# Attention with a long convolution beside it on one core: bounds in pairs, transform results copied whole, a fourth vector exponential, another order at the end

## The chip, the cores and the metric

The kernel runs on one core of one Trainium2 chip. The metric is the time on the device of one execution, in microseconds; the time of a kernel is the median of its runs. Engines: TensorE (PE for its matmuls, PEld for its weight loads), VectorE (DVE), ScalarE (ACT), GpSimd (POOL) and SyncE (SP); the last two mostly issue DMAs here.

## The reference

Two independent parts, each 2048 rows by 512 columns, side by side in the output:

```python
# A: attention, 32 heads of 16, one K and V for all heads
q = (x @ wq).reshape(B, S, H, Dh).transpose(0, 2, 1, 3)
k = x @ wk
v = x @ wv
scores = jnp.einsum("bhqd,bkd->bhqk", q, k) * (Dh ** -0.5)
o = jnp.einsum("bhqk,bkd->bhqd", softmax(scores), v)
a = o.transpose(0, 2, 1, 3).reshape(B, S, H * Dh) @ wo
# B: a causal convolution of 4 taps, a product, a causal convolution over
# the whole sequence (by transforms of length 4096), a gate
kv = shift(k, shift_k) * v
y = irfft(rfft(pad(kv)) * rfft(pad(ssm_k)))[:S] + kv * ssm_D
b = q * y
out = concatenate([a, b], axis=-1)
```

## The kernel before

**Attention.** The 32 heads times 2048 queries are cut into 32 stacks (`NQ`), numbered n: four heads and a chunk of 512 queries each. For a stack the kernel goes over 16 tiles of 128 keys (`NKT`), two heads of the stack at a time, so there are 32 turns to a stack. A turn emits the scores of one pair (`keys`, L934, eight matmuls in float16), the exponential of the pair on ScalarE (`exp`, L946, 128 partitions by 1024) and, later, the products with the values (`pv`, L970), which add up in PSUM over the stack. A turn of `attend` works two pairs ahead with scores and exponentials. The last stack goes through half its queries first, then the other half. At the end of a stack VectorE copies the two accumulators out (L979, L980), and the rows are stored; `heads` loads them back with the row sums (`rl`), takes reciprocals, spreads them through a DMA (`r`) and divides (L1076 to L1088); `wo_part` multiplies by `wo`. For stacks 30 and 31 the division is done in place by `over` (L1190 to L1201, six VectorE operations), and `last` writes the last rows of the output.

**The vector exponential.** For the stacks in `OWN_IN` the last key tile isn't given to ScalarE. Its scores go to PSUM, and VectorE makes the exponential by a polynomial (`own`): two reads of the scores for each of two head pairs (L1022, L1023), then for each pair one conversion (L1030) and five steps (L1033). TensorE then takes the values' products from there (L970, `f<-own`). Each such stack saves ScalarE two exponentials.

**The rest as fillers.** All other work (the projections of the queries, their bounds, the convolutions, the output projection) is cut into pieces by eight generator threads. Between the scores of two turns `_Fill.turn` puts in pieces as a small table of prices lets it: a turn has a budget of TensorE time (`SLOT` 916, `SCORES` 220, `PV` 430, `UNIT` 216 ns per unit of filler) and of VectorE time (each turn adds `RATE` 850 to a credit, and every piece takes its stated price off it). Groups of filler matmuls are two turns apart (`GAP`). A thread that comes earlier in the list is served first; `own` is the first. So the program is written in one order, and each engine works down its own list: a matmul that waits holds back all matmuls behind it. A piece that asks a different price, or is cut differently, moves every piece behind it.

**PSUM.** The scores use two pairs of banks, and another two pairs (`f`) hold one stack's accumulators and one filler group. A filler group can begin when VectorE has read the group before it.

**Transforms of the convolution.** `forward` (L284 to L289) and `backward` (L440 to L469) multiply by tables (`ft`: `ff` forward, `fi` backward) that GpSimd loads from memory a little ahead (`in_ff`, `in_fi`). Each group fills two banks, and VectorE copies or multiplies them out, one bank at a time.

**Bounds.** The exponentials are shifted by a bound made from the queries' size: for each of four groups of heads and each of four query chunks one matmul (L707) into 32 rows of a bank, a scaling (`gn`, L709), a maximum (`gm`, L729), and a DMA to the queries' rows in memory.

## Time and profile before

| | |
|---|---|
| median of 3 runs | 1016.74 us (1013.69 to 1018.21) |
| the profiled execution | 1014.1 us |
| its span | 1012.3 us |
| mean granted TensorE clock | 0.989 |
| TensorE matmuls, busy | 947.4 us, 94% |
| ScalarE, busy | 953.3 us, 94% |
| VectorE, busy | 738.7 us, 73% |
| GpSimd, busy | 172.0 us, 17% |

The profile is one execution. A group of instructions is told as line, engine, operation, output tile<-input tiles, count, then busy time and mean length of one, then the engine's idle time just before them with what ended it. In a row of a wait the numbers are the total, the times and the longest. In a row of a stretch they are its length, then the busy time (and count) of PE, PEld, DVE, ACT and POOL, the granted TensorE clock (1 is full speed), the share of the DMA engines and GB/s. In a row of the timeline they are start, length, engine and line; "[3.42 <-DMA ff<-in_ff]" says that the engine was idle for 3.42 us and that this load ended it.

### The profile page before, as it was taken

The page shows a single profiled execution, that of the slowest core. Times are in us where ns is not written, and L with a number is a line of the kernel's source. Part 1 is how long each engine was busy: PE and PEld are TensorE (multiplying, and loading weights), DVE is VectorE, ACT ScalarE, POOL GpSimd, SP SyncE. Part 2 cuts the span into 40 slices and gives each one's busy share as a digit, 9 for nine tenths or more (in the row PEclk, how much of TensorE's full clock was granted, in tenths as well). Part 3 has the DMA queues.
Part 4 walks back from the last instruction along what each step waited for, and adds up shares of the span by engine and source line. Part 5 has one row for each costly group of instructions (what it writes and reads, how often), then busy time and mean ns, then how long its engine had stood idle before and what let it go on. Part 6 is the DMA issues. An engine that isn't in the chain of part 4 may idle for free.

```text
span 1012.3 us, 51279 instructions
## 1 busy us (share of the span) xinstructions
PE 947.4 (94%) x23439; PEld 463.1 (46%) x23439; DVE 738.7 (73%) x1009; ACT 953.3 (94%) x1034; POOL 172.0 (17%) x305
## 2 busy tenths in 40 slices
PE   8999999999999999999999989999889989998985
PEld 4344455444454444445554545544334445443452
DVE  4647866998538888989988858598999942866633
ACT  4699999999999999999999989999999999999982
POOL 2443111411003000101233434000000023200000
PEclk9899999999999999999999999999999999999998
DMA  7262333432123211122154424101211143310101
GB/s 231 92 190 75 119 103 102 107 99 84 46 75 78 70 53 54 53 90 75 55 152 123 126 86 124 54 22 47 70 37 43 42 126 115 92 56 25 42 4 46
DMA packets 69317, 83.12 MB, mean 82 GB/s; under 512 B 20800, under 2 KB 58278, under 8 KB 69094
## 3 DMA queue, kind: packets, MB, share of 16 engines
q1 hardware_dynamic: 47142, 43.51, 13.6%
q0 software_dynamic: 20320, 35.46, 11.8%
q8 instruction: 185, 3.03, 1.3%
q10 hardware_dynamic: 1632, 0.81, 0.3%
q14 instruction: 38, 0.31, 0.1%
HBM read 54.66 MB, written 25.03 MB: 79 GB/s over the span
## 4 chain that ended last, share of the span: by engine, by line
PE 56%; ACT 27%; DVE 9%; issue 7%; DMA 2%; POOL 0%; SPq 0%; ACTq 0%; DVEq 0%; POOLq 0%
ACT p L946 26%; PE f L970 26%; PE s L934 16%; PE f L249 12%; DVE own L1033 2%; DVE sp L169 1%; DMA xb<-in_A_x 1%; DVE ao L979 1%; PE x L231 0%; PE f L617 0%; DVE u L218 0%; DVE sp L289 0%; DVE sp L219 0%; DVE sp L220 0%; DVE ao L980 0%
## 5 line engine op out<-in xcount | busy, mean ns | idle before, releaser
L946 ACT ACTIVATE p<-s 128x1024 f32<-128x1024 f32 x1018 | 940.8, 1068 | 22.2 <-PE s L934 19.3
L970 PE MATMUL f<-p,vx 64*32 64x512 f32 (+1 forms) x8896 | 554.0, 556 | 1.7 <-DVE cut L683 1.1
L934 PE MATMUL s<-st,kst 49*32 49x512 f16 x8144 | 431.0, 382 | 31.2 <-ACT p L946 27.6
L934 PEld LDWEIGHTS <-kst 49*32 49x32 f16 x8192 | 199.0, 89 | 396.5 <-issue 355.4
L970 PEld LDWEIGHTS f<-p,vx 64*32 64x32 f32 x8896 | 178.3, 106 | 30.0 <-issue 4.3
L169 DVE TENSOR_TENSOR sp<-sp 128x1024 f32<-128x1024 f32 x96 | 111.3, 1214 | 0.0
L289 DVE COPY sp<-f 128x512 f32<-128x512 f32 x64 | 41.2, 685 | 63.8 <-PE f L249 63.8
L294 POOL DMA_DIRECT2D ff<-in_ff x64 | 34.5, 544 | 284.4 <-ACT p L946 282.1
L249 PE MATMUL f<-wo,o 64*32 64x512 f16 x1440 | 57.4, 375 | 3.8 <-DVE r L467 1.6
L979 DVE COPY ao<-f 128x512 f32<-128x512 f32 (+1 forms) x33 | 22.2, 673 | 50.3 <-PE f L970 50.3
L169 DVE TENSOR_TENSOR sp<-sp,sp 128x1024 f32<-128x1024 f32 x48 | 55.9, 1213 | 0.2
L249 PE MATMUL f<-xT,wq 64*32 64x512 f16 x1344 | 51.8, 375 | 1.6 <-DVE gm L729 1.3
L294 POOL DMA_DIRECT2D fi<-in_fi x32 | 17.6, 555 | 187.1 <-ACT p L946 187.1
L249 PE MATMUL f<-a,ff 64*32 64x256 f32 x1024 | 43.4, 382 | 4.6 <-DMA ff<-in_ff 3.4
L467 DVE TENSOR_TENSOR r<-f,q 128x256 f32<-128x256 f32 x32 | 12.1, 419 | 45.2 <-PE f L249 45.2
L249 PE MATMUL f<-hT,ff 64*32 64x256 f32 x1024 | 41.5, 377 | 1.2 <-PE s L934 0.3
L249 PE MATMUL f<-sp,fi 64*32 64x256 f32 x1024 | 40.4, 376 | 0.4 <-PE s L934 0.4
L469 POOL DMA_DIRECT2D out<-r x32 | 17.5, 552 | 106.2 <-DVE r L467 105.9
L404 DVE TENSOR_TENSOR a<-a,t 128x512 f32<-128x512 f32 x48 | 33.2, 691 | 1.6
L395 DVE TENSOR_TENSOR t<-kk,tpb 128x512 f32<-128x512 f32 (+1 forms) x50 | 32.9, 662 | 0.7 <-DMA qd<-qp 0.7
L249 PEld LDWEIGHTS <-o 64*32 64x32 f16 x1440 | 22.5, 93 | 19.0 <-DVE r L467 2.1
L322 POOL DMA_DIRECT2D hin<-in_B_ssm_k x32 | 21.1, 665 | 58.8 <-ACT p L946 57.4
(165 smaller groups left out, 726.5 us busy)
## 6 DMA issues: line engine op xcount, KB each, us to landing
ff<-in_ff POOLq DMA_DIRECT2D x64, 128.0 KB, 2.7
od<-ao SPq DMA_DIRECT2D x60, 128.0 KB
qd<-qp SPq DMA_DIRECT2D x48, 128.0 KB
st<-qd SPq DMA_DIRECT2D x62, 98.0 KB
kk<-in_B_k POOLq DMA_DIRECT2D x32, 128.0 KB, 3.0
v<-in_B_v POOLq DMA_DIRECT2D x32, 128.0 KB, 3.2
hin<-in_B_ssm_k POOLq DMA_DIRECT2D x32, 128.0 KB, 5.5
fi<-in_fi POOLq DMA_DIRECT2D x32, 128.0 KB, 3.4
```

Of the source, the lines that this page charges most:

```text
L169: v.tensor_tensor(part(out), part(a), part(b), op)
L249: y = self.nc.tensor.matmul(out[j : j + 32, cols], w[r, j : j + 32], x[r], start=half == m == 0, stop=half == 1 and m == k - 1,)
L289: self.nc.vector.tensor_copy(c[:, :, m + i, :], b[i].rearrange("p (q n) -> p q n", q=2))
L294: self.paced(self.nc.gpsimd.dma_start(t[:, i], self.I[n][:, 2 * m2 + i]))
L322: self.paced(nc.gpsimd.dma_start(dst, src))
L395: nc.vector.tensor_tensor(out[:, n], kk[:, x], tap(i, n.stop - n.start), ALU.mult)
L404: nc.vector.tensor_tensor(a, a, t, ALU.add)
L934: self.nc.tensor.matmul(s[j : j + 32, e, :], self.kst[rows, k * P + j : k * P + j + 32], self.st[n][rows, a, cols], start=True, stop=True,)
L946: self.exps[u % 4] = self.nc.scalar.activation(self.pt[u], s, AF.Exp, scale=LN2 * DH**-0.5 / SC / SC)
L970: nc.tensor.matmul(self.acc[e][32 * j : 32 * j + 32, m], vx[rows, :], y, start=k == 0, stop=stop)
L979: nc.vector.tensor_copy(a, self.acc[0][:, m])
L1033: v.scalar_tensor_tensor(g, g if i < 4 else y, c[i], y if i else x.bitcast(BF16), ALU.add, ALU.mult)
```

## The change

Four edits.

- `OWN_IN` has 27 as well, so four stacks have a vector exponential.
- `halves` keeps its pair of banks as `self.both`; `forward` copies both banks in one instruction (128x1024 in place of two of 128x512) and `backward` multiplies both in one (128x512 in place of two of 128x256).
- `bounds` takes a tuple of one or two head groups: two matmuls go to rows 0 to 31 and 32 to 63 of one bank, and one `gn` and one `gm` read both. There are nine calls instead of sixteen; the DMAs stay one for each group.
- The end: the divisions of stack 30 (`lt`, two halves) and of the first half of stack 31 (`lr`) move from `wo_part` to the end of the thread `own`, which is served first, with a smaller step between looks (`WAIT, 0.5`). `last` puts the first matmul of the last output rows ahead of the final two value products, adds row block 0 on TensorE by an identity matmul, copies blocks 0 and 2 by ScalarE, adds block 1 on VectorE, and makes and stores block 3 in two halves.

Since the prices of the pieces are met earlier or later, the fillers from turn 83 on stand at other turns than before. The names of lines shift by three or more in the new program (L1033 is L1036, L294 is L295, L1088 is L1104).

GpSimd's queue where the second short convolution begins (stack 18): `out<-r` stores of the backward transform, loads `kk` and `v`, first forward tables `ff`. Before, then now:

```order
L469 DMA out<-r_13277 128x256 x2
L373 DMA kk_11516<-in_B_k 128x256 x2
L386 DMA v_13407<-in_B_v 128x256 x2
L373 DMA kk_11516<-in_B_k 128x256 x2
L386 DMA v_13621<-in_B_v 128x256 x2
L469 DMA out<-r_13393 128x256 x2
L294 DMA ff_13671<-in_ff 128x256 x2
L294 DMA ff_13674<-in_ff 128x256 x2
```

```order
L469 DMA out<-r_13125 128x256 x2
L374 DMA kk_11675<-in_B_k 128x256 x2
L387 DMA v_13286<-in_B_v 128x256 x2
L469 DMA out<-r_13283 128x256 x2
L295 DMA ff_13403<-in_ff 128x256 x2
L295 DMA ff_13406<-in_ff 128x256 x2
```

The first `ff` load stands after one `kk` and `v` pair where there were two. In turns: its issue was at 593 and its first matmul at 594; now they are at 581 and 586.

VectorE in stack 28, from the end of the second read of the scores (`own` from `f`) to the last step; `ao` is the accumulator's read, `r` the gate of the backward transform. Before, then now:

```order
L1023 SCALAR_TENSOR_TENSOR own_16575<-own_16574,f_19925 128x1024
L1030 TENSOR_SCALAR x_19936<-own_16574 128x1024
L1033 SCALAR_TENSOR_TENSOR own_16574<-own_16575 128x1024
L1033 SCALAR_TENSOR_TENSOR own_16574<-own_16574,own_16575 128x1024 x3
L1033 SCALAR_TENSOR_TENSOR own_16574<-own_16574,x_19936 128x1024
L1030 TENSOR_SCALAR x_20081<-own_16574 128x1024
L467 TENSOR_TENSOR r_19823<-f_20000,q_19443 128x256 x2
L979 COPY ao_20159<-f_19590 128x512
L980 TENSOR_TENSOR ao_20159<-ao_20159,f_19590 128x512
L1033 SCALAR_TENSOR_TENSOR own_16574<-own_16575 128x1024
L1033 SCALAR_TENSOR_TENSOR own_16574<-own_16574,own_16575 128x1024 x3
L1033 SCALAR_TENSOR_TENSOR own_16574<-own_16574,x_20081 128x1024
```

```order
L1033 TENSOR_SCALAR x_19946<-own_10601 128x1024
L1036 SCALAR_TENSOR_TENSOR own_10601<-own_10602 128x1024
L1036 SCALAR_TENSOR_TENSOR own_10601<-own_10601,own_10602 128x1024 x2
L982 COPY ao_20078<-f_19559 128x512
L983 TENSOR_TENSOR ao_20078<-ao_20078,f_19559 128x512
L1036 SCALAR_TENSOR_TENSOR own_10601<-own_10601,own_10602 128x1024
L1036 SCALAR_TENSOR_TENSOR own_10601<-own_10601,x_19946 128x1024
L467 TENSOR_TENSOR r_19833<-f_20010,q_19190 128x512
L1033 TENSOR_SCALAR x_20096<-own_10601 128x1024
L1036 SCALAR_TENSOR_TENSOR own_10601<-own_10602 128x1024
L1036 SCALAR_TENSOR_TENSOR own_10601<-own_10601,own_10602 128x1024 x3
L1036 SCALAR_TENSOR_TENSOR own_10601<-own_10601,x_20096 128x1024
```

The accumulator's read stands earlier in the chain, and `r` is one instruction. The second read is written at turn 889 and the products with the chain's end at 906; before, at 887 and 906. In the other stacks: 29 had 925 and 944, now 921 and 940; 30 had 959 and 976, now 951 and 968; 27 now has 857 and 876.

VectorE in stack 31, where `ao` is the accumulator's read, `wp` the rows of the last output block (from the group that TensorE makes with `wo`), and `lr` the six operations of `over`. Before, then now:

```order
L1171 SCALAR_TENSOR_TENSOR wp_20716<-f_22217,wp_20716 128x512
L1171 SCALAR_TENSOR_TENSOR wp_20717<-f_22217,wp_20717 128x512
L1195 STREAM_TRANSPOSE lr<-ao_22064 128x256
L1197 TENSOR_SCALAR lr<-lr 128x8
L1198 RECIPROCAL lr<-lr 128x8
L1199 COPY lr<-lr 128x256
L1200 STREAM_TRANSPOSE lr<-lr 128x256
L1201 TENSOR_TENSOR lr<-ao_22064,lr 128x256
L1195 STREAM_TRANSPOSE lr<-ao_22064 128x256
```

```order
L982 COPY ao_22011<-f_21400 128x512
L983 TENSOR_TENSOR ao_22011<-ao_22011,f_21400 128x512
L1201 STREAM_TRANSPOSE lr<-ao_22011 128x256
L1203 TENSOR_SCALAR lr<-lr 128x8
L1204 RECIPROCAL lr<-lr 128x8
L1205 COPY lr<-lr 128x256
L1206 STREAM_TRANSPOSE lr<-lr 128x256
L1207 TENSOR_TENSOR lr<-ao_22011,lr 128x256
L1187 SCALAR_TENSOR_TENSOR wp_20593<-f_21975,wp_20593 128x512
L1187 SCALAR_TENSOR_TENSOR wp_20594<-f_21975,wp_20594 128x512
L1201 STREAM_TRANSPOSE lr<-ao_22011 128x256
```

Before, both halves of `over` stood behind the last `wp` read of the `wo` groups; now the first half stands ahead of the first of those reads and the second half behind it. In turns: 998 to 1000 before, with the reader on TensorE at 999; now 987 to 989, with the reader at 997. The division of the first half of stack 31 stood behind all four `wp` adds after that (L1184), and now stands ahead of them (turn 1002).

The diff:

```diff
--- before.py
+++ after.py
@@ -68,7 +68,7 @@
 
 DOWN = 80
 OWN = NKT - 1
-OWN_IN = (28, 29, 30)
+OWN_IN = (27, 28, 29, 30)
 OWN_AT, OWN_PV = 14, 8
 
 
@@ -240,6 +240,7 @@
                 start = not banks
                 if start:
                     f = self.pair()
+                    self.both = f
                     banks += [f[:, 0, :], f[:, 1, :]]
                 for m in range(n, n + g // grain):
                     for e in range(2):
@@ -285,8 +286,8 @@
 
         work = [[(slice(CB * q, CB * q + CB), ft[:, i, q, :], src[:, i, :]) for q in range(2)] for i in range(2)]
         b = yield from self.halves(*work, 2, 1400)
-        for i in range(2):
-            self.nc.vector.tensor_copy(c[:, :, m + i, :], b[i].rearrange("p (q n) -> p q n", q=2))
+        out = c[:, :, m : m + 2, :].rearrange("p q i n -> p i q n")
+        self.nc.vector.tensor_copy(out, self.both.rearrange("p i (q n) -> p i q n", q=2))
 
     def table(self, n, m2):
         t = self.w.tile([P, 2, 2, P], F32, tag="ft", bufs=FT, name=self.nm(n))
@@ -463,8 +464,7 @@
                     x = cx[:, cc, 4 * g2[m // 4] + g1[m % 4], :]
                     work[i].append((cols, ft[m2][:, i, cc, :], x))
             b = yield from self.halves(*work, 2, 850)
-            for i in range(2):
-                nc.vector.tensor_tensor(r[:, i, :], b[i][:, cols], q[m2][:, i, :], ALU.mult)
+            nc.vector.tensor_tensor(r, self.both[:, :, cols], q[m2], ALU.mult)
             for i in range(2):
                 nc.gpsimd.dma_start(self.orr[:, 2 * m2 + i, D + blk * CB : D + (blk + 1) * CB], r[:, i])
 
@@ -700,14 +700,17 @@
         for r, part in ((0, 0), (DH, 1), (BR + 1, 0)):
             self.nc.sync.dma_start(self.qd[8 * g : 8 * g + 8, r : r + DH, c * 512 : (c + 1) * 512], qp[:, part, :])
 
-    def bound(self, g, c, b):
+    def bound(self, gs, c, b):
 
 
         nc, w = self.nc, self.w
-        nc.tensor.matmul(b[0:32, :], self.wb, self.qa[g, c], start=True, stop=True)
-        gn = w.tile([8, 512], F16, tag="gn", bufs=3, name=self.nm("gn"))
-        nc.vector.tensor_scalar(gn, b[0:8, :], -1.02 * SC * SC / ONE, -60000.0, ALU.mult, ALU.max)
-        nc.sync.dma_start(self.qd[8 * g : 8 * g + 8, BR, c * 512 : (c + 1) * 512], gn)
+        n = 32 * len(gs)
+        for i, g in enumerate(gs):
+            nc.tensor.matmul(b[32 * i : 32 * i + 32, :], self.wb, self.qa[g, c], start=True, stop=True)
+        gn = w.tile([n - 24, 512], F16, tag="gn", bufs=3, name=self.nm("gn"))
+        nc.vector.tensor_scalar(gn, b[0 : n - 24, :], -1.02 * SC * SC / ONE, -60000.0, ALU.mult, ALU.max)
+        for i, g in enumerate(gs):
+            nc.sync.dma_start(self.qd[8 * g : 8 * g + 8, BR, c * 512 : (c + 1) * 512], gn[32 * i : 32 * i + 8])
 
     def first_bound(self, b, a):
 
@@ -725,8 +728,9 @@
             r = slice(BR + 64 * e, BR + 64 * e + 1)
             self.nc.vector.tensor_scalar(st[r, a, :], b[r, e, :], f, -60000.0, ALU.mult, ALU.max)
 
-    def bound_max(self, g, c, b):
-        self.nc.vector.tensor_reduce(self.gm[0:16, 4 * c + g : 4 * c + g + 1], b[0:16, :], AX.X, ALU.max)
+    def bound_max(self, gs, c, b):
+        n = 32 * len(gs) - 16
+        self.nc.vector.tensor_reduce(self.gm[0:n, 4 * c + gs[0] : 4 * c + gs[0] + 1], b[0:n, :], AX.X, ALU.max)
 
     def prologue(self):
         nc = self.nc
@@ -824,12 +828,12 @@
             return 4
         return 5 if any(self.step >= x and ("wo", 4 * c) not in self.seen for c, x in enumerate(WO_AT)) else None
 
-    def bounds(self, g, c):
+    def bounds(self, gs, c):
         yield 2, 1400, NEW, 2
         b = self.bank()
-        self.bound(g, c, b)
-        self.bound_max(g, c, b)
-        self.qs.add((g, c))
+        self.bound(gs, c, b)
+        self.bound_max(gs, c, b)
+        self.qs.update((g, c) for g in gs)
 
     def rest_of_q(self):
         for c in range(2, 4):
@@ -837,7 +841,7 @@
             b = self.bank()
             self.kv_rows(self.kvt, c, b)
             self.k_chunk(c, b)
-        yield from self.bounds(0, 0)
+        yield from self.bounds((0,), 0)
         work = [y for dk in range(4) for y in self.three(self.wq[1][:, :, dk, :], self.xT[0][:, :, dk, :])]
         n = 0
         while n < 12:
@@ -862,9 +866,8 @@
                     cut = [self.q_cut(x) for x in b]
                     for i in range(2):
                         yield from self.q_parts(g + i, c, cut[i])
-                for h in range(g + (c == g == 0), g + 2):
-                    yield WAIT, 2
-                    yield from self.bounds(h, c)
+                yield WAIT, 2
+                yield from self.bounds((1,) if c == g == 0 else (g, g + 1), c)
             if c == 0:
                 for g in range(4):
                     yield 0, 700
@@ -1033,6 +1036,19 @@
                     v.scalar_tensor_tensor(g, g if i < 4 else y, c[i], y if i else x.bitcast(BF16), ALU.add, ALU.mult)
             self.owed = [(-1 - n, part) for part in range(2)]
         self.seen.add("own")
+        yield from self.after(("cx", 1))
+        both = self.w.tile([P, 2, 4, 512], F32, tag="in", bufs=1, name="lr")
+        self.lt, self.lr = both[:, 0], both[:, 1]
+        while self.slot < 2 * NKT * (NQ - 1) + 1:
+            yield WAIT, 0.5
+        for h in range(2):
+            yield 0, 1800
+            self.over(self.ao2[:, 256 * h : 256 * h + 256], self.lt, h)
+        self.seen.add("lt")
+        while self.slot < 2 * NKT * (NQ - 1) + NKT:
+            yield WAIT, 0.5
+        yield 0, 1800
+        self.over(self.ao[:, 0:256], self.lr, 0)
 
     def attend(self, fill):
         self.od = self.dr.tile([NQ, P, 512], F32, name="od")
@@ -1169,23 +1185,13 @@
             b = yield from self.wo_rows(i, [14], 1400)
             for r in range(2):
                 nc.vector.scalar_tensor_tensor(self.wp[i + r], b[r], 1 / (OS * WS), self.wp[i + r], ALU.mult, ALU.add)
-        both = w.tile([P, 2, 4, 512], F32, tag="in", bufs=1, name="lr")
-        t, self.lr = both[:, 0], both[:, 1]
-        for h in range(2):
-            while self.slot < 2 * NKT * (NQ - 1) + 1:
-                yield WAIT, 1
-            yield 0, 1800
-            self.over(self.ao2[:, 256 * h : 256 * h + 256], t, h)
+        yield from self.after("lt")
         halves = [slice(256 * h, 256 * h + 256) for h in range(2)]
         for i in (0, 2):
-            work = [[(h, t[:, 2, r * P : (r + 1) * P], self.wl[0][:, h]) for h in halves] for r in (i, i + 1)]
+            work = [[(h, self.lt[:, 2, r * P : (r + 1) * P], self.wl[0][:, h]) for h in halves] for r in (i, i + 1)]
             b = yield from self.halves(*work, 2, 1400)
             for r in range(2):
                 nc.vector.tensor_tensor(self.wp[i + r], self.wp[i + r], b[r], ALU.add)
-        while self.slot < 2 * NKT * (NQ - 1) + NKT:
-            yield WAIT, 1
-        yield 0, 1800
-        self.over(self.ao[:, 0:256], self.lr, 0)
 
     def over(self, a, t, h):
 
@@ -1206,24 +1212,29 @@
         xr = self.out.rearrange("b (c p i) d -> (b c) p i d", c=4, p=P, i=4)
         fill.finish()
         t = self.w.tile([P, 2, 4, 512], F32, tag="big", bufs=2, name="lb")[:, 0]
-        self.pv(len(self.at) - 2, None)
-        s = [self.wide()[:, 0, :]]
         y = [self.s2("y", (512,)) for _ in range(4)]
         rows = lambda x, i: x[:, 2, i % 2 * P : (i % 2 + 1) * P]
-        self.mm(s[0], rows(self.lr, 0), self.wl[1])
+        b = self.pair()
+        s = [b[:, 0, :], b[:, 1, :]]
+        self.mm(s[0], rows(self.lr, 0), self.wl[1], stop=False)
+        self.pv(len(self.at) - 2, None)
         self.pv(len(self.at) - 1, None, True)
         self.over(self.ao[:, 256:512], t, 0)
-        s += [self.wide()[:, 0, :], self.wide()[:, 0, :], self.bank()]
+        self.mm(s[0], self.ident, self.wp[0], start=False)
         self.mm(s[1], rows(self.lr, 1), self.wl[1])
+        s += [self.wide()[:, 0, :], self.wide()]
         self.mm(s[2], self.ident, self.wp[2], stop=False)
-        for i in range(2, 4):
-            self.mm(s[i], rows(t, i), self.wl[1], start=i > 2)
-        for i in range(2):
-            nc.vector.tensor_tensor(y[i], self.wp[i], s[i], ALU.add)
+        self.mm(s[2], rows(t, 2), self.wl[1], start=False)
+        nc.scalar.copy(y[0], s[0])
+        nc.sync.dma_start(xr[3][:, 0, 0:D], y[0])
+        nc.vector.tensor_tensor(y[1], self.wp[1], s[1], ALU.add)
+        nc.sync.dma_start(xr[3][:, 1, 0:D], y[1])
         nc.scalar.copy(y[2], s[2])
-        nc.vector.tensor_tensor(y[3], self.wp[3], s[3], ALU.add)
-        for i in range(4):
-            (nc.sync, nc.scalar)[i // 2 % 2].dma_start(xr[3][:, i, 0:D], y[i])
+        nc.scalar.dma_start(xr[3][:, 2, 0:D], y[2])
+        for i, h in enumerate((slice(0, CB), slice(CB, D))):
+            self.mm(s[3][:, i, 0:CB], rows(t, 3), self.wl[1][:, h])
+            nc.vector.tensor_tensor(y[3][:, h], self.wp[3][:, h], s[3][:, i, 0:CB], ALU.add)
+            nc.sync.dma_start(xr[3][:, 3, h], y[3][:, h])
 
 
 class _Fill:
```

## The prediction

> **What bounds the kernel now.** I read the page first (busy shares, the chain of work that ended last, the costliest groups), then the waits of TensorE, then busy time by stretches, one stretch per stack, and last the timeline of the two places where the pace broke most.
>
> ```profile
> PE 947.4 (94%) x23439; PEld 463.1 (46%) x23439; DVE 738.7 (73%) x1009; ACT 953.3 (94%) x1034; POOL 172.0 (17%) x305
> PE 56%; ACT 27%; DVE 9%; issue 7%; DMA 2%; POOL 0%; SPq 0%; ACTq 0%; DVEq 0%; POOLq 0%
> L946 ACT ACTIVATE p<-s 128x1024 f32<-128x1024 f32 x1018 | 940.8, 1068 | 22.2 <-PE s L934 19.3
> ```
>
> ScalarE's 1018 exponentials set the pace: 940.8 us of busy time are 0.924 us each, 1068 ns long and overlapping their neighbours. Outside the start and the end ScalarE stood idle only 22.2 us, nearly all of it waiting for scores. TensorE is as busy (94%), but its matmuls are written in order and one that must wait blocks the scores behind it. So the body can lose time only by fewer exponentials or fewer waits of TensorE. These are the waits that matter, us in total, times, longest:
>
> ```profile
> PE f L249 <- DMA ff<-in_ff: 3.4, 1, 3.4
> PE x L231 <- issue: 2.5, 1, 2.5
> PE f L249 <- DVE gm L729: 2.3, 4, 1.0
> PE f L249 <- issue: 2.2, 1, 2.2
> PE f L249 <- DVE r L467: 1.6, 1, 1.6
> PE f L970 <- DVE cut L683: 1.1, 1, 1.1
> PE f L249 <- DVE wp L1140: 1.0, 1, 1.0
> PE f L970 <- DVE own L1033: 0.6, 1, 0.6
> ```
>
> By stretch (length, then busy PE, PEld, DVE, ACT, POOL, granted clock), the three stacks with a vector exponential (28, 29, 30), stack 31, and the stretch of stack 18 that holds the DMA wait:
>
> ```profile
> 872.20:901.80 29.60, 28.84 (x736) 14.58 (x721) 18.05 (x24) 29.55 (x33) 5.37 (x10) 1.00 0.27 82
> 901.80:932.80 31.00, 28.72 (x736) 13.46 (x736) 20.92 (x23) 29.56 (x34) 2.08 (x4) 1.00 0.08 26
> 932.80:963.50 30.70, 28.02 (x720) 13.17 (x719) 22.77 (x27) 29.77 (x33) 0.00 (x0) 1.00 0.17 46
> 963.50:993.30 29.80, 26.88 (x880) 16.84 (x864) 9.12 (x23) 26.20 (x29) 0.00 (x0) 0.94 0.02 4
> 575.00:600.00 25.00, 21.34 (x521) 11.88 (x512) 12.34 (x24) 20.15 (x22) 9.68 (x19) 0.93 0.34 106
> ```
>
> ScalarE idled 0.05, 1.44 and 0.93 us in the three stacks (2.4 together), 3.60 us in stack 31 and 4.85 us around 590.
>
> **One exponential fewer per round of keys.** Adding stack 27 to the list takes two exponentials off ScalarE, 2 x 0.92 = -1.8 us. TensorE's score and value matmuls of that tile stay; its 94% could cover the gain, but the row of stack 28, which already has the list's treatment, shows ScalarE 29.55 of 29.60, so ScalarE sets the pace there. Bounds -1.8 and 0.
>
> **What the added chain costs.** VectorE reads the two key groups and then runs twelve dependent operations, in stack 30:
>
> ```profile
> 935.14 1.22 DVE L1023 SCALAR_TENSOR_TENSOR own<-own,f 128x1024 f32<-128x1024 f32 x1
> 948.94 1.23 DVE L1033 SCALAR_TENSOR_TENSOR own<-own,x 128x1024 f32<-128x1024 f32 x1
> ```
>
> From the second read's end, 936.36, to 950.17 are 13.8 us; with that group's two reads of 1.22 each, 16.3. Before, the second read was written 19, 19 and 17 turns ahead of the value matmuls that need the chain's end, in stacks 28, 29, 30; now 19, 17, 19, 17 in 27 to 30. At 0.92 us seventeen turns are 15.6, nineteen 17.4. The old stack 28 had an accumulator read (two of 0.69, near 1.4) and a gated store (0.7) inside its chain: 18.4 against 17.4, and ScalarE idled 0.05, so up to 1.0 us of slack lies between writing and need. The old stack 30 had none inside but the read just ahead: 16.3 against 15.6, and it idled 0.93. Now stack 28 has 18.4 against 15.6, late by 2.8 less 0 to 1.0, and I take 2.3; stack 30 has the read inside, 17.7 against 15.6, and I take 1.5; 27 and 29, at nineteen turns with two or three reads in their way, I put between the old 0.05 and 1.44 and on the upper side, since more reads stand inside: 0.9 each. That is 5.6 us, against 2.4 measured for three: +3.2. The lower bound goes by the rows alone (19 turns idled 0.05 and 1.44, 17 turns 0.93: 2 x 0.75 + 2 x 0.93 = 3.4, so +1.0); the upper lets each be late without slack (2.8 + 2.1 + 1.4 + 0.8), +4.7. I take +3.2, since both 17-turn chains now carry what the measured one did not.
>
> Such a stall can also halve TensorE's clock:
>
> ```profile
> 910.55:913.96 3.41, 2.13 (x64) 0.84 (x47) 3.38 (x5) 3.33 (x4) 0.00 (x0) 1.00 0.02 5
> 972.02:975.43 3.41, 1.38 (x52) 1.07 (x60) 3.10 (x11) 0.97 (x2) 0.00 (x0) 1.00 0.00 0
> 975.43:978.84 3.41, 3.41 (x80) 2.10 (x72) 0.45 (x2) 2.35 (x3) 0.00 (x0) 0.50 0.02 5
> 589.73:593.14 3.41, 1.31 (x36) 0.99 (x44) 2.74 (x5) 0.10 (x1) 1.31 (x3) 1.00 0.54 172
> 593.14:596.55 3.41, 3.41 (x56) 2.32 (x48) 0.00 (x0) 2.37 (x3) 0.00 (x0) 0.50 0.02 7
> ```
>
> The clock is granted in windows of 3.41 us. After a window in which TensorE was busy 40% or 38% the next ran at half; after 62% it did not. In a half window ScalarE is busy 2.35 to 2.37 of 3.41, so one costs about 1.05 us. A wait of 2.3 us inside one window leaves 1.1 of 3.41, under 40%; cut by a window's edge it does nothing. I leave it out of the sum and put it in the range. The Trainium skill (TensorE: Matmul & The Clock Gate, "Why this matters for your kernels") asks only for no idle gaps above about 3 us. Here a gap of 2.2 us was followed by half clock, so the trace differs. By the page the own stalls could never halve the clock; by the rows one in two of 2.3 us may, about +0.5 us on the sum.
>
> **The table in stack 18.** The first tables of the second short transform:
>
> ```profile
> 588.91 2.13 POOL L294 DMA_DIRECT2D ff<-in_ff  x4
> 591.83 0.68 PE L249 MATMUL f<-a,ff 64*32 64x256 f32 x12 [3.42 <-DMA ff<-in_ff]
> 593.04 1.02 ACT L946 ACTIVATE p<-s 128x1024 f32<-128x1024 f32 x1 [3.43 <-PE s L934]
> ```
>
> Issue to landing is 591.83 - 588.91 = 2.9 us, and the matmul stood one turn behind the issue. In the new order the issue stands at turn 581 and the matmul at 586, five turns or 4.6 us, and the queue ahead of it is shorter by one load of `kk` and one of `v`. Of the 4.85 us (with the half window that followed) I take -4.4, leaving 0.5 for VectorE's `a`, which is made in the same turns; bounds -4.85 and 0.
>
> **Stack 31.** VectorE made both halves of `over` for the row block of stack 30 only behind TensorE's last `wo` group, and TensorE then waited 2.2 us for them (the wait put down to issue) and paid a half window. Now the first half stands ahead of that group's read and the second right behind it, eight turns before the matmul that needs them. -3.3 of 3.60; bounds -3.6 and -2.2.
>
> **Copies and bounds.**
>
> ```profile
> L289 DVE COPY sp<-f 128x512 f32<-128x512 f32 x64 | 41.2, 685 | 63.8 <-PE f L249 63.8
> L467 DVE TENSOR_TENSOR r<-f,q 128x256 f32<-128x256 f32 x32 | 12.1, 419 | 45.2 <-PE f L249 45.2
> L1022 DVE TENSOR_SCALAR own<-f 128x1024 f32<-128x1024 f32 x6 | 7.3, 1222 | 3.3 <-PE f L934 3.3
> L709 DVE TENSOR_SCALAR gn<-f 8x512 f16<-8x512 f32 x16 | 10.7, 672 | 5.5 <-PE f L707 5.5
> ```
>
> Thirty-two pairs of copies become one each: 2 x 0.685 = 1.37 to 1.22 (the row with the same shape from the same memory), 4.8 us of VectorE; sixteen pairs of products 0.84 to 0.69, 2.4; seven bounds fewer, 7 x 1.34 = 9.4. These hide behind ScalarE, at 73% VectorE, except where TensorE waited: `gm` 2.3 us at four of sixteen bounds. Half the bounds are gone, -1.1 (bounds -2.3, 0). The bounds' DMAs stay sixteen. What the re-timed fillers give back elsewhere, read by the same sums at turns 204, 366, 421, 460, 524 and 782, is 4.2 turns or 3.9 us less 0.3 at each of six places, against the 1.1 + 1.0 that stood at `cut` and `wp`: about +0.5 (bounds -2 and +3).
>
> **The end.**
>
> ```profile
> 984.00 9.31 ACT L946 ACTIVATE p<-s 128x1024 f32<-128x1024 f32 x10
> 995.57 1.65 PE L231 MATMUL x<-wl,lr 128*32 128x512 f32 x8 [2.46 <-issue]
> 997.15 1.11 PE L970 MATMUL f<-p,vx 64*32 64x256 f32 x16
> 1001.02 0.42 DVE L1201 TENSOR_TENSOR lb<-ao,lb 128x256 f32<-128x256 f32 x1
> 1002.18 1.45 PE L231 MATMUL x<-wp,ident 128*32 128x512 f32 x8 [2.39 <-DVE y L1222]
> 1003.33 2.01 PE L231 MATMUL x<-wl,lb 128*32 128x512 f32 x8
> 1006.72 0.69 DVE L1224 TENSOR_TENSOR y<-wp,f 128x512 f32<-128x512 f32 x1 [4.08 <-PE f L231]
> ```
>
> The last exponential ends at 993.31, the last value matmul 4.95 later at 998.26, `lb` 3.2 after that, `y[3]` at 1007.41, the span 4.9 later: 19.0 us. Between exponential and value matmul stood `over`, done by VectorE after the last `wp` add, with TensorE idle 2.46. Now `over` is written twelve turns ahead. What stays is the `wl,lr` matmul, at full clock half of 1.65, then value matmuls of about 1.2: 2.0 instead of 4.95. `lb` again 3.2. Then 2.0 for the third row block, and for the fourth two halves in series, 0.8 + 0.42 each: 4.4 against 5.97 (the identity matmul no longer waits for `y`). Store 4.9. That is 14.5, so -4.5; bounds -6.0 (all at full clock) and -3.0 (the first matmul waits for the `wp` add that frees its bank, and the ScalarE store lands last).
>
> **The sum.** -1.8 + 3.2 - 4.4 - 3.3 - 1.1 + 0.5 - 4.5 = -11.4. The profiled execution took 1014.1, 2.6 under the median of 1016.74 and near the lowest run; -11.4 gives 1002.7 for it and 1005.3 for the median, which I forecast as 1005.
>
> **Rivals.**
> A, own chains: all four late by the upper bound and a half window behind two of them: -11.4 + 1.5 + 2.1 = -7.8, 1009. For it: every chain now has other reads in it. Against: before, nineteen turns cost nothing in stack 28.
> B, the stall in stack 18 moves instead of going: another table or `a` is late where the fillers now stand, 4.4 comes back: -7.0, 1010. For it: every filler from turn 83 on is re-timed. Against: the leads of the tables I could read are five turns or more.
> C, slower: row sums. The re-timed `wo` heads now load the row sums, or the broadcast of them, one to four turns ahead of VectorE's use at seven places in stacks 22 to 30, and behind it VectorE queues what frees TensorE's banks.
>
> ```profile
> DVE o L1088 <- DMA r<-rd: 2.0, 1, 2.0
> DVE rl L1076 <- DMA rl<-od: 1.3, 1, 1.3
> ```
>
> Before these cost VectorE 2.0 and 1.3 us, nothing of it on TensorE. Were all seven to stop TensorE, 2.4 us each with a half window, 3.45, they would give +24, 1029; it turns slower from 7 x 2.4 = 17 on. Against it: the last of them, with the shortest lead, has no reader for twelve turns.
> D, no change in what the code says: the end doesn't shorten (the moved matmul waits for `wp`, then half clock) and the two exponentials are covered by TensorE: -11.4 + 4.5 + 1.8 = -5.1, 1012.
>
> **Chances.** The forecast 0.58, A 0.14, B 0.12, D 0.08, C 0.08. About 0.5%, 5.1 us, is what a measurement of this kernel can tell from no change. The forecast and A and B lie beyond it on the fast side, except a tail of them (0.06); D is half and half; C is slower but for the smaller waits. Faster 0.79, same 0.12, slower 0.09. The low end takes the good bounds of the chain (+1.0 for +3.2), the end (-6.0 for -4.5) and the re-timing (-2 for +0.5): -17.6, 999. The high end takes in A, B and D with half a microsecond over: 1013.
>
> **What would show it.** In the new profile: 1016 exponentials; no wait on `ff` near 590; ScalarE busy all but 0.5 us of stack 31; the last exponential some 14.5 us before the end; waits of TensorE on `own` and `r` in stacks 27 to 30 near 5.6 us. It is wrong if waits of over 2 us stand anywhere else between turns 83 and 850, or if the row sums (C) appear among what TensorE waits for.

## The result and the profile after

The changed kernel takes 1004.97 us (median of 5 runs, 1004.58 to 1006.74) against 1015.88 us for the kernel before (5 runs, 1013.69 to 1018.21): ratio 0.9895, 95% interval 0.9877 to 0.9913. Run again in a later job it took 1005.25 against 1015.96 (0.9897, 0.9873 to 0.9920). The profiled execution took 1004.97, with a span of 1003.1 where that of the kernel before was 1012.3. One execution in all that follows, of the kernel with the pairs of bounds alone, ran at a granted clock of 0.651 and took 1340.87; it is left out of that kernel's median.

From the page of the changed kernel, busy shares, chain and the costliest group:

```profile
PE 941.7 (94%) x23471; PEld 459.7 (46%) x23471; DVE 744.6 (74%) x963; ACT 951.4 (95%) x1033; POOL 172.7 (17%) x305
PE 51%; ACT 25%; DVE 14%; issue 6%; DMA 2%; SPq 0%; POOL 0%; ACTq 0%; DVEq 0%
L949 ACT ACTIVATE p<-s 128x1024 f32<-128x1024 f32 x1016 | 938.3, 1067 | 18.4 <-PE s L937 16.3
```

Two exponentials fewer, each as long as before, and ScalarE's idle time before them went from 22.2 to 18.4 us. VectorE's part of the chain that ended last rose from 9% to 14%. TensorE's waits, where they bear on the prediction:

```profile
PE f L973 <- DVE own L1036: 3.0, 3, 1.7
PE f L910 <- DVE sp L290: 1.5, 1, 1.5
PE f L250 <- DVE sp L290: 1.2, 1, 1.2
PE f L250 <- DVE gm L733: 1.2, 3, 0.5
PE f L973 <- DVE cut L683: 1.1, 1, 1.1
PE f L250 <- DVE cut L683: 0.9, 1, 0.9
PE f L250 <- issue: 0.5, 1, 0.5
```

The wait for `ff` is gone, and so is the one for `over` in stack 31 (issue, 2.2): the issue wait of 0.5 that is listed stands at 186 us, in a group of the queries' projection. `gm` fell from 2.3 to 1.2. The waits for the vector exponential are 3.0 in all, where there was one of 0.6; those for `sp`, 0.2 and 0.3 before at two lines, are 1.5 and 1.2; a second one for `cut` is new. By stretch, the stacks 27 to 31, then the one in stack 18:

```profile
841.70:870.00 28.30, 26.23 (x672) 13.21 (x656) 19.72 (x20) 27.66 (x31) 6.43 (x12) 1.00 0.24 75
870.00:901.50 31.50, 28.30 (x712) 13.83 (x704) 22.56 (x25) 29.59 (x33) 4.30 (x8) 1.00 0.21 69
901.50:931.80 30.30, 28.76 (x736) 14.31 (x729) 23.46 (x23) 29.67 (x34) 3.16 (x6) 1.00 0.11 36
931.80:962.50 30.70, 29.46 (x792) 14.46 (x776) 18.73 (x25) 29.57 (x33) 0.00 (x0) 1.00 0.16 45
962.50:988.70 26.20, 24.82 (x864) 16.12 (x848) 11.14 (x27) 25.87 (x29) 0.00 (x0) 1.00 0.02 5
577.20:605.50 28.30, 27.47 (x736) 14.03 (x720) 24.00 (x38) 27.89 (x31) 14.45 (x28) 1.00 0.49 150
```

ScalarE idles 0.64, 1.91, 0.63 and 1.13 us in stacks 27 to 30, 0.33 in stack 31 (3.60 before) and 0.41 around stack 18. Of the signs that the prediction named, one is off: TensorE's waits for `own` and `r` in stacks 27 to 30 come to 3.5 us (3.0 and 0.5), not 5.6. The end, from the timeline:

```profile
982.17 6.58 ACT L949 ACTIVATE p<-s 128x1024 f32<-128x1024 f32 x7
988.93 1.06 PE L231 MATMUL f<-wl,lr 128*32 128x512 f32 x8 [0.96 <-issue]
989.93 1.09 PE L973 MATMUL f<-p,vx 64*32 64x256 f32 x32
993.78 0.43 DVE L1207 TENSOR_TENSOR lb<-ao,lb 128x256 f32<-128x256 f32 x1
994.26 1.50 PE L231 MATMUL x<-wl,lb 128*32 128x512 f32 x16 [0.53 <-DVE lb L1207]
997.01 0.42 DVE L1236 TENSOR_TENSOR y<-wp,x 128x256 f32<-128x256 f32 x1 [0.76 <-PE x L231]
```

The last exponential ends at 988.75, the last value matmul at 991.02, `lb` at 994.21, the last add at 997.43, the span at 1003.10.

One measure serves the rest of the text. From the starts of the exponentials in a trace I take, for each stack, what its turns lasted beyond 0.917 us apiece, and call it the stack's loss. From the kernel before to the changed one, in us, with the profile of the repeated run of the changed kernel beside it:

| | before | after | difference | after, repeated |
|---|---|---|---|---|
| exponentials, 1018 and 1016 at 0.917 | 933.5 | 931.7 | -1.8 | 931.7 |
| first exponential starts | 30.6 | 32.2 | +1.5 | 32.4 |
| loss of stack 0 | 5.2 | 5.2 | 0.0 | 7.0 |
| loss of stack 18 | 5.4 | 0.8 | -4.6 | 1.6 |
| loss of stacks 27 to 30 | 3.0 | 5.2 | +2.3 | 5.2 |
| loss of stack 31 | 4.3 | 0.5 | -3.8 | 0.5 |
| loss of all other stacks | 11.2 | 13.1 | +1.9 | 10.9 |
| from the last exponential's end to the end | 19.0 | 14.4 | -4.7 | 14.2 |

Together -9.2, as the spans have it. The row of the other stacks is the least certain: between two executions of one program it differs by 2.2. The start isn't touched by the change: in the other profiles below it is anywhere from 30.8 to 32.4, and stack 0 loses 5.1 to 7.0.

### The profile page after: what moved, and what is told of

Same layout as the page of the kernel before. It is cut to its first block, busy times and chain, and to the rows that moved or that the text cites. A ratio compares the mean times of both kernels' runs of the same rounds, so it can differ in the third digit from the quotient of the medians.

```text
span 1003.1 us, 51275 instructions
## 1 busy us (share of the span) xinstructions
PE 941.7 (94%) x23471; PEld 459.7 (46%) x23471; DVE 744.6 (74%) x963; ACT 951.4 (95%) x1033; POOL 172.7 (17%) x305
## 3 DMA queue, kind: packets, MB, share of 16 engines
q1 hardware_dynamic: 47430, 43.78, 13.7%
## 4 chain that ended last, share of the span: by engine, by line
PE 51%; ACT 25%; DVE 14%; issue 6%; DMA 2%; SPq 0%; POOL 0%; ACTq 0%; DVEq 0%
ACT p L949 25%; PE f L973 24%; PE s L937 14%; PE f L250 11%; DVE own L1036 3%; DVE sp L169 1%; DVE ao L982 1%; DMA xb<-in_A_x 1%; DVE sp L290 1%; DVE ao L983 1%; DMA qd<-qp 1%; DVE sp L435 0%; PE f L617 0%; DVE own L1025 0%; DVE t L435 0%
## 5 line engine op out<-in xcount | busy, mean ns | idle before, releaser
L949 ACT ACTIVATE p<-s 128x1024 f32<-128x1024 f32 x1016 | 938.3, 1067 | 18.4 <-PE s L937 16.3
L973 PEld LDWEIGHTS f<-p,vx 64*32 64x32 f32 x8880 | 175.8, 106 | 30.1 <-issue 4.6
L290 DVE COPY sp<-f 128x1024 f32<-128x1024 f32 x32 | 39.1, 1223 | 64.9 <-PE f L250 64.8
L295 POOL DMA_DIRECT2D ff<-in_ff x64 | 34.7, 546 | 277.1 <-ACT p L949 275.6
L982 DVE COPY ao<-f 128x512 f32<-128x512 f32 (+1 forms) x33 | 22.2, 674 | 56.7 <-PE f L973 56.6
L295 POOL DMA_DIRECT2D fi<-in_fi x32 | 17.8, 562 | 180.4 <-ACT p L949 180.4
L250 PE MATMUL f<-a,ff 64*32 64x256 f32 x1024 | 41.2, 378 | 0.7 <-DVE a L407 0.6
L467 DVE TENSOR_TENSOR r<-f,q 128x512 f32<-128x512 f32 x16 | 11.0, 689 | 41.2 <-PE f L250 41.2
```

What stands on the lines that cost most here:

```text
L250: y = self.nc.tensor.matmul(out[j : j + 32, cols], w[r, j : j + 32], x[r], start=half == m == 0, stop=half == 1 and m == k - 1,)
L290: self.nc.vector.tensor_copy(out, self.both.rearrange("p i (q n) -> p i q n", q=2))
L295: self.paced(self.nc.gpsimd.dma_start(t[:, i], self.I[n][:, 2 * m2 + i]))
L949: self.exps[u % 4] = self.nc.scalar.activation(self.pt[u], s, AF.Exp, scale=LN2 * DH**-0.5 / SC / SC)
L973: nc.tensor.matmul(self.acc[e][32 * j : 32 * j + 32, m], vx[rows, :], y, start=k == 0, stop=stop)
L982: nc.vector.tensor_copy(a, self.acc[0][:, m])
```

## The experiments

Each is compared with the kernel before as it ran in the same job (medians 1014.84, 1014.47 and 1015.96).

**The end alone.** The kernel before with `own`, `wo_part` and `last` from the changed kernel, and three stacks in the list:

```diff
+        for h in range(2):
+            yield 0, 1800
+            self.over(self.ao2[:, 256 * h : 256 * h + 256], self.lt, h)
...
-            self.over(self.ao2[:, 256 * h : 256 * h + 256], t, h)
...
-        self.pv(len(self.at) - 2, None)
-        s = [self.wide()[:, 0, :]]
...
+        self.mm(s[0], rows(self.lr, 0), self.wl[1], stop=False)
+        self.pv(len(self.at) - 2, None)
```

> The kernel before with only the end reordered (the divisions moved to the first thread, and the new last step). All fillers up to stack 30 stand where they stood. My theory: the waits of stack 31 (3.3) and the end (4.5) go, and nothing else does: -7.8, 1008; the wait for the table in stack 18 stays at 3.4. Rival: the end is bound by the last store, and only stack 31 gains, -3.3, 1012.5.

Measured: 1007.14, -7.7 (ratio 0.9922, 0.9889 to 0.9954). In its trace stack 31 loses 0.6 where it lost 4.3, the end is 14.3 long where it was 19.0, and stack 18 still loses 5.1. The theory holds in each part; the rival (a gain in stack 31 alone) is out.

**The copies alone.** The kernel before with `halves`, `forward` and `backward` from the changed one.

```diff
-        for i in range(2):
-            self.nc.vector.tensor_copy(c[:, :, m + i, :], b[i].rearrange("p (q n) -> p q n", q=2))
+        out = c[:, :, m : m + 2, :].rearrange("p q i n -> p i q n")
+        self.nc.vector.tensor_copy(out, self.both.rearrange("p i (q n) -> p i q n", q=2))
```

> The kernel before with only the whole copies and products of the transforms. No filler moves. My theory: 7 us of VectorE time are saved, all of it beside ScalarE: 0 to -0.7, 1015 to 1016, with the waits for r and the copies a little shorter. Rival: VectorE's saturated stacks 11 to 25 give the time on: -3 or more. Rival on the other side: a copy of two banks holds the banks longer, +1 or more.

Measured: 1014.19, -0.65 (ratio 0.9992, 0.9974 to 1.0011), no difference that this measurement can tell. The costs on VectorE are as the prediction had them (in the changed kernel the wide copy takes 1223 ns, the wide product 689), and they are hidden, or nearly: in its trace the stacks other than 0, 18 and 27 to 31 lose 9.8 where they lost 11.2, a gain of 1.4 that the total can't show.

**The pairs of bounds alone.** The kernel before with `bound`, `bound_max`, `bounds` and the calls from the changed one.

```diff
-                for h in range(g + (c == g == 0), g + 2):
-                    yield WAIT, 2
-                    yield from self.bounds(h, c)
+                yield WAIT, 2
+                yield from self.bounds((1,) if c == g == 0 else (g, g + 1), c)
```

> The kernel before with only the paired bounds. In its order every filler from turn 83 on stands where it stands in the changed kernel, so the issue of the first table of stack 18 is five turns ahead of its use. My theory: it gains the table's 4.4 and about 1.1 at the bounds, and loses 0.5 elsewhere and about 2 at the three chains (17, 19, 16 turns): -3, 1013. Rival 1: a bound's VectorE time is worth something by itself, 9.4 us of it saved: -5 or more. Rival 2: the order is worth nothing and the wait comes back elsewhere: 0.

Measured: slower, 1018.47 (seven runs, 1015.13 to 1026.24; ratio 1.0040, 1.0003 to 1.0077), which is just clear of no difference. My theory missed, and so did both rivals. The gain in stack 18 is there, 5.4 to 1.1, and stack 31 loses 1.9 less; but stacks 28 to 30 lose 7.9 in place of 3.0, and the stacks that I had put at -0.6 lose 3.3 more. The stretches of stacks 28 and 29, in which ScalarE idles 1.65 and 3.33 us:

```profile
873.80:905.00 31.20, 28.60 (x732) 14.06 (x723) 24.24 (x29) 29.55 (x33) 3.14 (x6) 1.00 0.17 52
905.00:938.00 33.00, 29.78 (x736) 13.69 (x721) 18.25 (x20) 29.67 (x33) 0.00 (x0) 0.95 0.09 25
```

TensorE's waits of this kernel name what the prediction priced too low:

```profile
PE f L973 <- DVE own L1036: 3.1, 2, 1.7
PE f L249 <- DVE wp L1160: 2.1, 1, 2.1
PE f L910 <- DVE sp L289: 1.7, 1, 1.7
```

The 2.1 us in stack 29 is no wait for the chain's end: the last read of a `wo` group stands inside the chain on VectorE, as VectorE's timeline has it:

```profile
914.34 2.48 DVE L1036 SCALAR_TENSOR_TENSOR own<-own,own 128x1024 f32<-128x1024 f32 x2
916.74 1.28 DVE L1160 TENSOR_SCALAR wp<-f 128x512 f32<-128x512 f32 x2
917.94 1.22 DVE L1036 SCALAR_TENSOR_TENSOR own<-own,x 128x1024 f32<-128x1024 f32 x1
```

TensorE's next `wo` group needs that group's banks, and it stands ahead of the products. A half window followed, that is, one window of 3.41 us at half clock (0.95 over the stretch). So a chain delays two kinds of work: its own products, and whatever else VectorE must read while it runs.

**Stack 27 taken out again.**

```diff
-OWN_IN = (27, 28, 29, 30)
+OWN_IN = (28, 29, 30)
```

> The changed kernel with the vector exponential in stacks 28, 29, 30 alone (27 taken back out). My theory: two exponentials more cost 1.8 us, and stack 27's wait goes; the fillers behind turn 850 stand otherwise, with the chains' second reads now 17, 19 and 16 turns ahead of their products, so TensorE still waits 4 to 5 us for them. Net 1 us slower than the changed kernel: 1006, still about 10 us under the kernel before. Rival (the fourth chain costs more than it saves, since it crowds VectorE): 1003 or less.

Measured: 1009.65, -5.2 (ratio 0.9946, 0.9925 to 0.9967, where the changed kernel has 0.9895, 0.9877 to 0.9913), so the fourth chain is worth some 5 us, not 1, and doesn't cost more than it saves, as the rival had it. Two exponentials are 1.8 of it. The rest is the order: without 27 the second reads stand 17, 19 and 16 turns ahead of the products as in the kernel with the pairs alone, and the same waits are there:

```profile
PE f L973 <- DVE own L1036: 3.1, 2, 1.7
PE f L250 <- DVE wp L1173: 2.1, 1, 2.1
```

Stacks 27 to 30 lose 7.8 here and 5.2 with the fourth chain. The chain of 27 moves the later ones to 17, 19 and 17 turns and brings a gated store in place of the `wo` read that blocked.

**Neither pairs nor stack 27.** The kernel before with the copies and the end. (The pairs can't be taken out with 27 left in the list: fillers are then left over at the end of the order.)

> The changed kernel without the paired bounds and without stack 27 (which does not fit without them): the kernel before with the whole copies and the new end. My theory: -7.7 and -0.6 add up, since neither moves a filler: -8.3, 1006.5, with stack 18 still losing 5 us and stacks 28 to 30 losing 2.7. That is 3 us under the kernel with the pairs and three stacks (1009.65), so the pairs alone cost time. Rival: the pairs pay and it comes out at 1010 or more.

Measured: 1007.63, -6.8 (ratio 0.9926, 0.9904 to 0.9948). The two parts add up within the interval (-7.7 and -0.65), with stack 18 losing 6.5 and stacks 28 to 30 losing 2.9. It stands 2 us under the kernel with the pairs and three stacks, as expected, with intervals that overlap.

**The table's lead.** In the kernel before, six turns between the issue of the first tables and the first request for their matmuls:

```diff
         ft = {i: self.table("ff", i) for i in range(2)}
+        yield WAIT, 3
         for m2 in range(8):
```

> The kernel before with six turns of waiting put behind the issue of the first tables of each short transform, so that their first use stands four turns later (598 for 594). My theory: ScalarE's loss of 5.4 us in stack 18 goes to under 1.0, whatever else the moved fillers do; the three chains now stand 17 turns ahead of their products each, where they stood 19, 19 and 17, and lose some 2 to 3 us more than the 2.7 before. Net -2, 1013. Rival: the table is late because the queue of GpSimd or the memory is busy, and then stack 18 still loses 3 us or more.

Measured: 1014.62, no change (ratio 0.9993, 0.9971 to 1.0014). The stretch of stack 18, in the kernel before and here:

```profile
572.00:605.00 33.00, 29.29 (x736) 16.16 (x720) 19.08 (x34) 28.15 (x32) 12.13 (x23) 0.95 0.37 113
```

```profile
574.00:603.80 29.80, 29.09 (x753) 15.07 (x743) 18.44 (x33) 29.70 (x34) 12.09 (x23) 1.00 0.40 125
```

ScalarE idles 0.10 us in place of 4.85, the wait for `ff` isn't among TensorE's, and the stack loses 0.5 in place of 5.4. The queue ahead of the tables is the same as before, and in the kernel before these loads took 2.6 to 2.8 us from issue to landing, where the median of all 64 is 2.7. So the lead was the whole cause, and queue or memory being busy is out. The total doesn't show it because the three chains moved to 17 turns each and lose 7.0 in place of 3.0. I had put that at 2 to 3.

**No vector exponential.**

```diff
-OWN_IN = (27, 28, 29, 30)
+OWN_IN = ()
```

> The changed kernel with no vector exponential at all, 1024 exponentials on ScalarE. My theory: eight exponentials more cost 7.3 us, and stacks 27 to 30 lose under 1 us in place of 5.2: +3, 1008. Rival A: the chains' stalls eat all they save: 1005. Rival B: they cost nothing: 1012.

Measured: 1005.41, -9.1 (ratio 0.9903, 0.9864 to 0.9942), near rival A. From 842.5 to 960 us ScalarE idles 0.02:

```profile
842.50:960.00 117.50, 107.18 (x2656) 50.41 (x2641) 17.89 (x29) 117.48 (x129) 10.66 (x20) 1.00 0.16 52
```

Eight exponentials more are 7.3 us, and all losses together are 4.9 less. So the four chains as they stand buy some 2 us by these two sums, and neither the spans of the profiles (1002.9 here, 1003.1 and 1003.6 with the chains) nor the times (-9.1 here, -10.9 and -10.7 with them) can tell that from nothing.

**The products later.** The changed kernel, with a wait before the chain's result is handed over:

```diff
+            yield WAIT, 1
             self.owed = [(-1 - n, part) for part in range(2)]
```

> The changed kernel with the products that take the vector exponential two turns later (a wait of two turns before they are handed over). Nothing else is changed. My theory: the chains are late by 0.7 to 2.0 us against their products, so two turns, 1.8 us, take away most of the 4.0 us that stacks 28 to 30 lose at those products: -3.5, 1001.5. Rival: VectorE is simply full there, and the stall moves to the next read in its list (a wo group or the accumulator): 1005.

Measured: 1007.37 (ratio 0.9921, 0.9888 to 0.9954), its five runs from 1003.31 to 1009.83; that is no faster than the changed kernel. Theory and rival are both half right. The wait for `own` is gone from TensorE's list and stacks 28 and 29 lose under 0.3 each, in place of 2.1 and 0.9. But in stack 30 `_Fill.turn` put a `wo` group into the turn that the products left, and it waits for the read behind the chain:

```profile
PE f L250 <- DVE wp L1174: 2.5, 1, 2.5
```

Stack 30 loses 4.1 with a half window, in place of 1.3. The next kernel therefore leaves stack 30 as it was, and gives 28 four turns and 27 and 29 two:

```diff
+            yield WAIT, 1.5 if n == 28 else 0.5
             self.owed = [(-1 - n, part) for part in range(2)]
```

The half step stands in the code for stack 30 too, but its products stay where they were in TensorE's list, 17 turns behind the second read; those of 27, 28 and 29 are now 21 turns behind.

> The changed kernel with the products of the vector exponential later by four turns in stack 28 and two in 27 and 29, and left in place in stack 30, where moving them let a wo group in ahead that then waited for VectorE. My theory: stacks 28 and 29 lose under 0.4 us each in place of 2.1 and 0.9, stack 30 keeps 1.3: -2.6 against the changed kernel of the same job, some 1002.5. Rival: the wait moves again, to a wo group or to the accumulator's read, and the two come out within 1 us.

> The changed kernel once more, on the same chip as the next one: 1005, its stacks 28, 29 and 30 losing 2.1, 0.9 and 1.3 us again, since its order is fixed. In stack 13 the half window (1.0 of the 2.9 us there) comes or not with the phase of the clock's windows.

Measured in one job: 1001.59 (ratio 0.9856, 0.9831 to 0.9881) and the changed kernel again 1005.25. That is 3.7 us less, of which the traces have 3.2 in stacks 27 to 30 (5.2 to 2.0), and 14.4 less than the kernel before. By stretch, stacks 28 and 29 and the first of 30:

```profile
872.20:901.50 29.30, 27.77 (x715) 13.65 (x704) 22.45 (x26) 29.30 (x33) 4.29 (x8) 1.00 0.23 74
901.50:930.50 29.00, 27.70 (x728) 13.66 (x720) 22.94 (x23) 29.00 (x33) 3.16 (x6) 1.00 0.12 38
```

ScalarE is never idle there, with VectorE as busy as in the changed kernel (22 to 23 us). So VectorE wasn't full: its results were asked for too early. Asked for later, the four chains seem to pay: ratio 0.9856 against 0.9903 without any, though the intervals (0.9831 to 0.9881 and 0.9864 to 0.9942) still overlap. In the repeated run of the changed kernel the losses of stacks 28, 29 and 30 were 2.11, 0.89 and 1.34 again (2.11, 0.90, 1.34 the first time), and stack 13 lost 1.3 in place of 2.9: 0.9 of that is the half window there, which didn't come, and the wait ahead of it took 0.6 less.

## Why the prediction was right, and where not

The forecast for the median was 1005, and 1004.97 came, inside the range. That they meet so closely is luck: the five runs lie between 1004.58 and 1006.74. Term by term, against the table above:

- **Two exponentials, -1.8.** As said; ScalarE sets the pace.
- **Chains, +3.2.** +2.3, between the bounds. Stack 28 was put at 2.3 and lost 2.1, stack 30 at 1.5 and lost 1.3, stack 29 at 0.9 and lost 0.9. Stack 27 lost 0.9, but 0.8 of that was a wait ahead of the chain's products. One row was read wrongly: the 1.44 of the old stack 29 was taken for a chain that was late, but TensorE waited there 1.6 us with a `wo` group for the gated store inside the chain (`PE f L249 <- DVE r L467: 1.6`, in the prediction's list), at 914.3 us, and not for the chain's end. So the kernel before already showed the second kind of wait that a chain brings.
- **Table, -4.4.** -4.6 (-3.8 in the repeated run), and the lead shown to be the cause.
- **Stack 31, -3.3.** -3.8.
- **End, -4.5.** -4.7. Its pieces were off and cancelled: from the last exponential to the last value matmul 2.3 (2.0 forecast), `lb` 3.2 as forecast, from there to the last add 3.2 (4.4 forecast, with half clock that didn't come), and 5.7 from there to the end (4.9 forecast).
- **Bounds and re-timing, -0.6 together.** This is the step that failed in its parts: +1.9 in the first profile, -0.3 in the repeated one. The `gm` part is right (2.3 to 1.2, -1.1). "What the re-timed fillers give back elsewhere", put at +0.5, was about +3 in the first profile. As it is written its sum even gives 0: 3.9 less 0.3 at each of six places is 2.1, against 1.1 + 1.0. The places were the ones named: turns 204, 366, 421, 460, 524 and 782 lost 1.2, 0.8, 2.0, 1.2, 0.8 and 0.7, together 6.7 (6.1 in the repeated run) where I had counted 2.1; and the half window behind 421 added 0.9. Against it stand the old places at 357, 549, 657 and 814, which lost 3.5 together and are gone; those at 332 and 666, another 1.3, are waits for `gm`. That makes +4.1. The whole copies, which the prediction put at nothing, take 1.4 off these stacks in the two profiles that have them in the old order (9.8 and 9.8, against 11.2 in the kernel before and with the end alone). In the six profiles that have the copies and the order of the pairs the loss is 10.9 to 13.7, in the mean 12.3. So on the mean the pairs' order takes 2.5, `gm` included, and the copies give more than half of it back.
- **The start, not in the sum:** +1.5 in the one profile, and no part of the change.

So the mechanisms of the large terms are right, and the total is right partly by luck. In the first profile the terms' errors (+2.5 there, -0.9, -0.2, -0.5 and -0.2 in the others) leave +0.7 and the start adds 1.5, which gives -9.2 for the forecast -11.4; the medians moved by 10.9. What the terms could not show is which edit pays, since the fillers' order was taken as given. By the runs: the end -7.7, the copies -0.65, the pairs of bounds about +4, and the fourth chain some -5 on top of the pairs. The pairs bring the table's 4.4 and lose more than that elsewhere; only with the fourth chain, which fits because of them, do they pay back.

Of the rivals, A (the chains late, two half windows; 1009) is near in its number for the kernel with the pairs and three stacks, where the chains' waits, a `wo` group's wait and one half window make it up, and not for the changed one. B and D didn't occur. C neither: the new order does keep VectorE waiting 6.1 us for the row sums' broadcast in stack 30, with the shortest lead, and nothing on TensorE waits behind it, as argued.

## What to carry to other kernels

Where one engine sets the pace and the work of the others is written in a fixed order around it, an edit acts first through the places that it moves: an edit that takes 9 us off an engine at 73% can cost 4. Compare the turn at which a result is made with the turn at which it is asked for, edit by edit, and look also at what else the making engine must read in between. A stall of the consumer beside a producer that isn't full is mended by asking later, and then by looking at what slips into the place that is left.

## What the runs showed of the hardware

The prediction had three windows to go by; the twelve profiles have more. In each profile all changes of the granted clock lie on one grid of 3.413 us. Between 60 and 985 us I took TensorE's busy share in each window of that grid that ran at full speed, and the clock of the next window. At 45% busy or less the next window was at half speed in 10 of 10; from 48 to 53% in 3 of 9; above 53% in none of 3207. A window at half speed was followed by a second one once in 14 times (76% busy, in stack 18 of the kernel with the copies and the end). One of each in the changed kernel, the window and the one after it:

```profile
427.76:431.17 3.41, 1.77 (x48) 0.80 (x55) 3.38 (x6) 3.16 (x4) 0.00 (x0) 1.00 0.35 107
431.17:434.58 3.41, 3.41 (x64) 1.78 (x56) 3.34 (x6) 1.61 (x2) 0.00 (x0) 0.50 0.14 38
881.73:885.14 3.41, 1.73 (x44) 0.67 (x36) 3.31 (x5) 2.24 (x3) 0.00 (x0) 1.00 0.37 126
885.14:888.55 3.41, 3.41 (x102) 2.09 (x93) 0.14 (x1) 2.67 (x3) 0.00 (x0) 1.00 0.06 10
```

Both were about half busy (52 and 51%), and only the first was followed by half clock. So gaps that add up to some 1.7 us in 3.4 can be enough. The same waits cost the half window in one execution and not in another, as the grid doesn't start with the program: in the repeated run its edges stand at 426.67, 430.08 and 433.49, the same waits are shared out over two windows (85 and 65% busy), and no half window follows. The Trainium skill (TensorE: Matmul & The Clock Gate, "What's actually happening") has the free-running window of about 3.4 us, and the trace agrees; it gives the half rate as what follows at least one idle window, and there the trace differs, since a window that is half busy can do.
